# Squares of the rows taken in the expert stage from a second load, no longer tile by tile in attention

## The chip, the core and the metric

The kernel runs on one core of one Trainium2 chip. The time is device microseconds of one execution of the whole program. TensorE (PE) multiplies matrices, VectorE (DVE), ScalarE (ACT) and GpSimd (POOL) work elementwise, SyncE (SP) issues most DMAs. Each engine takes its instructions in the order in which the program lists them.

## What is computed

Sliding-window attention (batch 8, 8 heads, 576 positions, head size 64, window 64), and over its rows a mixture of eight experts that sends each row to one of them:

```python
x = attn_out.transpose(0, 2, 1, 3).reshape(4608, 512)
xn = x / (np.linalg.norm(x, axis=-1, keepdims=True) + 1e-06)
en = expert_emb / (np.linalg.norm(expert_emb, axis=-1, keepdims=True) + 1e-06)
logits = xn @ en.T / tau
expert_idx = np.argmax(logits, axis=1)
gate_w = softmax(logits)[np.arange(N), expert_idx]
h = np.maximum(x[mask] @ w1[e], 0.0)               # 512 -> 1024
out[mask] = gate_w[mask, None] * (h @ w2[e])       # 1024 -> 512
```

The expert is chosen from logits that are not yet divided by the row's norm, since the norm does not move the maximum. The norm, the root of the row's sum of squares, is needed only for the gate.

## The kernel before

Every engine's order is written out by hand. There are two parts that overlap for some 30 us.

**Attention**, 36 tiles of 128 rows, one stage per tile (`stages(s)`), software pipelined: stage s makes the scores of tile s, turns the probabilities of tile s-1, multiplies them with the values for tile s-2, and turns the finished rows of tile s-3. On ScalarE a stage runs, in this order: `own_scores(s)` (L262, a copy from PSUM), the copy of the turned probabilities (`attn_copy`, L295), the copy of the turned rows (`xT_evac`, L384), `squares(s-3)` (L371), at the end of a group of four tiles a small copy of the logits in PSUM (`four_beside`, L416), the issue of a load of keys, and `exponentials(s)` (L276). VectorE merges the scores (L265), takes the maximum (L269), masks probabilities (L298), and divides the rows of tile s-2 (`x_out`, L359 to L363). POOL subtracts the maximum (`less_max`, L273), masks (L301) and scatters finished rows with `place` (L522). In some stages ScalarE and VectorE also split a piece of the first weights (L676, L677).

A finished row is 528 numbers: 512 features, 8 logits (from column `C_LOG`), the sum of squares (`C_SS`) and the token's number (`C_TOK`). `squares(T)` is an activation that writes 512 throw-away values `sq` and leaves their sum in column `C_SS` of the row. `place` writes the rows to DRAM (`xs`), sorted by expert.

**Expert stage**: groups of slots of 128 sorted rows, 39 slots in 13 groups here (kinds E, D, C, F, H with 2, 4, 3, 2 and 1 slots; groups 0 and 1 are E, 2 to 7 are D). Matrices are split into a high and a low half for three passes. For each slot SP loads the 512 features in four DMAs in an order that VectorE can transpose (`load_x`, L890) and the last 16 columns with logits, sum of squares and token into `rest` (`load_rest`, L896). For each group it loads w1 and w2 (`load1` L992, `load2` L1001). In `group(g)` layer 1 runs in parts (8 for a D group); each part's result, in one of four PSUM buffers `ph`, goes through ScalarE's relu to `hh` (L1040) and VectorE's low half `hl` (L1044). Behind the first four parts stands the split of w2 (`renew`, L198 and L201), behind a later part the issue of the next w2 and the gates (`gates`). Layer 2 runs slot by slot (L1084) with the work for the next group between the slots (`ahead`: transposes, split of w1, high and low half of x). `finish` scales a slot's result by its gate on ScalarE (L1109) and scatters it from POOL (L1112); `loads(g + 2)` ends the group.

Gates are made for a batch of slots at once, the first batch being the four slots of groups 0 and 1: `gate_root` (L941) takes the power 0.5 on POOL, `gate_logits` (L947 to L963) is a chain of nine VectorE instructions, `gate_exp` (L968) is on ScalarE, `gate_out` (L978 to L982) again on VectorE. At the seam between attention and experts the order is written line by line (L1284 to L1427): there `gate_root(0)` stands ahead of layer 1 of group 1, and behind the work for group 2 come `gate_logits(0)`, `gate_exp(0)`, `gate_out(0)`, `finish` of group 0's slots, and layer 2 of group 1.

## Time and profile before

| | |
|---|---|
| three runs | 605.72, 606.02, 606.87 us (median 606.02) |
| profiled execution | 605.96 us, span from first to last instruction 604.2 us |
| busy share of the span | TensorE 96%, weight loads 83%, VectorE 60%, ScalarE 48%, POOL 41% |
| mean granted TensorE clock | 0.996 of full speed |
| chain that ended last | TensorE 74%, issue 7%, POOL 6%, VectorE 5%, DMA 4%, ScalarE 3% |

Times in rows are microseconds from the first instruction unless ns stands beside them. `out<-in` are the program's names for tiles, with buffer numbers left out. In a timeline a bracket `[0.52 <-ACT odd L416]` says that the engine was idle for 0.52 us before this instruction and which instruction ended the wait. PEld is TensorE's loading of weights, SPq the sequencer of SP. L with a number is a line of the kernel.

### The profile page before, as it was taken

The numbers are of one execution on the slowest core, as the hardware profiler recorded it, in microseconds if no ns is written. First come the engines' busy times: TensorE is split into PE (matmuls) and PEld (weight loads), VectorE is DVE, ScalarE is ACT, GpSimd is POOL, SyncE is SP. The second block draws the span as 40 slices with busy tenths as digits, with TensorE's granted clock in tenths as the row PEclk, the third lists the DMA queues.
The fourth block names the chain that finished last, engine by engine and source line by source line (L and its number), as shares of the span: only waits on it lengthen the run. The fifth ranks groups of instructions, "written<-read, shape, count | busy, mean of one in ns | idle before, by whom it ended". The sixth has DMA issues, their size and how long they took to land.

```text
span 604.2 us, 16147 instructions
## 1 busy us (share of the span) xinstructions
PE 582.1 (96%) x6198; PEld 500.6 (83%) x6198; DVE 364.1 (60%) x880; ACT 292.5 (48%) x519; POOL 245.0 (41%) x230
## 2 busy tenths in 40 slices
PE   8999998899899999999999999999999999999995
PEld 7888787778889888888888888888888999989984
DVE  5777887888679766166076066166255373728583
ACT  3677776677441464145155145235244363436362
POOL 3558888787822432313214115105204233113221
PEclk9999999999999999999999999999999999999998
DMA  8988988786333796734644554445346455565730
GB/s 281 291 252 269 296 265 290 244 275 190 148 113 135 209 313 199 215 121 123 175 133 136 143 151 141 123 157 173 89 132 204 109 161 145 174 186 178 233 95 23
DMA packets 72471, 110.11 MB, mean 182 GB/s; under 512 B 14773, under 2 KB 34997, under 8 KB 72384
## 3 DMA queue, kind: packets, MB, share of 16 engines
q1 hardware_dynamic: 62080, 80.88, 45.9%
q0 software_dynamic: 6000, 19.18, 8.2%
q10 hardware_dynamic: 4304, 8.93, 4.8%
q8 instruction: 50, 0.82, 0.6%
q14 instruction: 37, 0.30, 0.2%
HBM read 89.69 MB, written 20.05 MB: 182 GB/s over the span
## 4 chain that ended last, share of the span: by engine, by line
PE 74%; issue 7%; POOL 6%; DVE 5%; DMA 4%; ACT 3%; SPq 0%; POOLq 0%; ACTq 0%; DVEq 0%
PE ph L1023 35%; PE po L1084 33%; POOL aM L301 2%; POOL xs L522 2%; DMA out<-o,rest 2%; POOL sm L273 1%; PE back L285 1%; DVE aM L298 1%; DVE xr L363 1%; DVE sm L265 1%; PE odd L321 1%; PE even L335 1%; PE xback L403 1%; PE odd L335 1%; PE score L255 1%
## 5 line engine op out<-in xcount | busy, mean ns | idle before, releaser
L1044 DVE SCALAR_TENSOR_TENSOR hl<-ph,hh 128x512 fp32r<-128x512 f32 (+2 forms) x84 | 54.1, 647 | 154.2 <-ACT hh L1040 154.2
L1023 PE MATMUL ph<-xh,w1h 128*128 128x512 f32 (+2 forms) x384 | 132.5, 345 | 1.3 <-DVE rk L503 1.3
L1023 PE MATMUL ph<-xl,w1h 128*128 128x512 f32 (+2 forms) x384 | 131.9, 344 | 0.0
L1023 PE MATMUL ph<-xh,w1l 128*128 128x512 f32 (+2 forms) x384 | 131.9, 344 | 0.0
L921 POOL TENSOR_TENSOR xl<-xt,xh 128x512 fp32r<-128x512 f32 x37 | 61.8, 1669 | 166.2 <-ACT xh L917 165.8
L1084 PE MATMUL po<-w2l,hh 128*128 128x512 f32 x312 | 121.7, 390 | 0.3 <-DVE w2l L201 0.3
L1084 PE MATMUL po<-w2h,hh 128*128 128x512 f32 x312 | 121.9, 391 | 0.0
L1084 PE MATMUL po<-w2h,hl 128*128 128x512 f32 x312 | 121.6, 390 | 0.0
L1040 ACT ACTIVATE hh<-ph 128x512 fp32r<-128x512 f32 (+2 forms) x84 | 47.5, 566 | 132.9 <-PE ph L1023 121.3
L1112 POOL DMA_INDIRECT out<-o,rest x39 | 43.4, 1112 | 131.4 <-ACT o L1109 106.9
L1023 PEld LDWEIGHTS ph<-xh,w1h 128*128 128x128 f32 x384 | 72.0, 188 | 9.2 <-issue 1.4
L1023 PEld LDWEIGHTS ph<-xl,w1h 128*128 128x128 f32 x384 | 72.1, 188 | 7.9 <-POOL xl L921 0.2
L1023 PEld LDWEIGHTS ph<-xh,w1l 128*128 128x128 f32 x384 | 72.1, 188 | 7.5
L1084 PEld LDWEIGHTS po<-w2l,hh 128*128 128x128 f32 x312 | 58.6, 188 | 13.1 <-DVE w2l L201 1.2
L1084 PEld LDWEIGHTS po<-w2h,hl 128*128 128x128 f32 x312 | 58.6, 188 | 12.3
L1084 PEld LDWEIGHTS po<-w2h,hh 128*128 128x128 f32 x312 | 58.6, 188 | 11.9
L201 DVE TENSOR_TENSOR w1l<-w1raw,w1h 128x1024 fp32r<-128x1024 f32 x44 | 60.4, 1379 | 9.9 <-ACT w1h L198 9.9
L201 DVE TENSOR_TENSOR w2l<-w2raw,w2h 128x1024 fp32r<-128x1024 f32 x48 | 58.8, 1224 | 11.9 <-ACT w2h L198 11.9
L1109 ACT ACTIVATE o<-po,gate 128x512 f32<-128x512 f32 (+1 forms) x39 | 26.5, 684 | 52.4 <-PE po L1084 46.9
L198 ACT CAST w2h<-w2raw 128x1024 fp32r<-128x1024 f32 x48 | 50.1, 1043 | 0.0
L273 POOL TENSOR_TENSOR sm<-sm,st 128x512 f32<-128x512 f32 x36 | 37.4, 1038 | 28.3 <-DVE st L269 26.7
L198 ACT CAST w1h<-w1raw 128x1024 fp32r<-128x1024 f32 x44 | 45.7, 1045 | 3.7 <-DMA w1raw<-in_w 3.7
(225 smaller groups left out, 820.4 us busy)
## 6 DMA issues: line engine op xcount, KB each, us to landing
w2raw<-in_w SPq DMA_DIRECT2D x44, 512.0 KB, 3.8
w1raw<-in_w SPq DMA_DIRECT2D x40, 512.0 KB, 4.4
xb<-xs SPq DMA_DIRECT2D x156, 64.0 KB, 2.2
v<-in_v SPq DMA_DIRECT2D x36, 260.0 KB, 4.1
qT<-in_q SPq DMA_DIRECT2D x36, 256.0 KB, 3.8
kT<-in_k ACTq DMA_DIRECT2D x26, 256.0 KB, 4.2
kT<-in_k SPq DMA_DIRECT2D x10, 256.0 KB, 6.4
w1raw<-in_w SPq DMA_DIRECT2D x8, 256.0 KB, 4.7
```

The costliest lines, as they stand in the source:

```text
L198: nc.scalar.copy(hi[c], raw[c])
L201: eng.tensor_tensor(out=lo[c], in0=raw[c], in1=hi[c].bitcast(F32), op=ALU.subtract)
L273: nc.gpsimd.tensor_tensor(out=t, in0=t, in1=st.pop(T).unsqueeze(2).to_broadcast([P, 8, WIN]), op=ALU.subtract)
L301: nc.gpsimd.tensor_tensor(out=aM[T][:, 0], in0=aM[T][:, 0], in1=halves[:, 0].unsqueeze(1).to_broadcast([P, 4, P]), op=ALU.mult)
L335: nc.tensor.matmul(px[T][hp][pz, u * (D + 1):(u + 1) * (D + 1)], lhsT=mine[pr, u, pz], rhs=vblock(g)[pr, u], start=u == 0 and first[0] and ...
L921: eng.tensor_tensor(out=xl, in0=t, in1=xh.bitcast(F32), op=ALU.subtract)
L1023: nc.tensor.matmul(o, lhsT=ww[c][:, f * P:(f + 1) * P], rhs=xx[:, c, :n], start=(c == 0 and i == 0), stop=(c == 3 and i == 2))
L1040: nc.scalar.activation(hh, ph[g, part][:, :parts(g) * rows_of(g)], AF.Relu)
L1044: nc.vector.scalar_tensor_tensor(out=hl, in0=ph.pop((g, part))[:, :parts(g) * rows_of(g)], scalar=0.0, in1=hh.bitcast(F32), op0=ALU.max, o ...
L1084: nc.tensor.matmul(o, lhsT=xx, rhs=ww[f // 2][:, f % 2], start=(f == 0 and k == 0), stop=(f == 7 and k == 2))
L1109: nc.scalar.activation(o[:, :w], y[:, :w], AF.Copy, scale=gate[:, at:at + 1])
L1112: d = nc.gpsimd.indirect_dma_start(out=out, out_offset=bass.IndirectOffsetOnAxis(ap=tok, axis=0), in_=o, in_offset=None, bounds_check=N - ...
```

## The change

The 36 squares leave the attention stages, and column `C_SS` of the rows is zeroed. In the expert stage each slot's rows are loaded a second time, whole and in plain order, into one of four buffers `xw` (`load_whole`, one DMA of 128 x 512 numbers behind the slot's `load_rest`), and ScalarE squares them from there, with the sum in a small tile `norm` from which the gates read. For group g+1 the squares stand in the second half of group g's layer 1, one behind each part. For the first four slots and the four of group 2 loads and squares stand at the seam, and `gate_root(0)` moves behind them.

```diff
--- before.py
+++ after.py
@@ -365,10 +365,6 @@
     def tokens(G):
         a, b = GROUPS[G]
         nc.gpsimd.tensor_copy(x_rows(a, b)[:, :, C_TOK].bitcast(I32), ct[:, a:b])
-
-    def squares(T):
-        sq = ap.tile([P, DM], BF16, name="sq", bufs=1)
-        nc.scalar.activation(sq, xr[T][:, :DM], AF.Square, accum_out=xr[T][:, C_SS:C_SS + 1])
 
     xT, pxT = {}, {}
 
@@ -633,8 +629,6 @@
         if s - 4 in (28, 29):
             nc.scalar.copy(x_rows(s - 4, s - 3)[:, 0, C_LOG:C_LOG + E], side[(s + 1) % 2][:, :E])
         less_max(s)
-        if there(3):
-            squares(s - 3)
         for G in four:
             four_beside(G)
         load_k(s + RK - 1, nc.sync if s < 6 else nc.scalar)
@@ -895,6 +889,19 @@
         for a in slots:
             note(a, nc.sync.dma_start(rest[:, column(a)], rows(a)[:, DM:ROW]))
 
+    def load_whole(*slots):
+
+        for a in slots:
+            whole[a] = take("xw")
+            note(a, nc.sync.dma_start(whole[a], rows(a)[:, :DM]))
+
+    def squares(*slots):
+
+        for a in slots:
+            nc.scalar.activation(junk, whole.pop(a), AF.Square, accum_out=norm[:, column(a):column(a) + 1])
+
+    whole = {}
+
     def x_turned(a):
 
         b = xb.pop(a)
@@ -937,7 +944,7 @@
         a0, a1 = BATCH[k]
         t, m, t0, t1 = gk[k] = [take("gin")[:, :a1 - a0]] + [take("gsm")[:, :a1 - a0] for _ in range(3)]
         at = slice(column(a0), column(a0) + a1 - a0)
-        gk[k] += [rest[:, at, :E], rest[:, at, C_SS - DM]]
+        gk[k] += [rest[:, at, :E], norm[:, at]]
         nc.gpsimd.tensor_tensor(out=t1, in0=gk[k][5], in1=half.to_broadcast([P, a1 - a0]), op=ALU.pow)
 
     def gate_logits(k):
@@ -1152,6 +1159,7 @@
             for a in SLOT[g]:
                 load_x(a)
             load_rest(*SLOT[g])
+            load_whole(*SLOT[g])
 
     def group(g):
 
@@ -1171,6 +1179,8 @@
                 settle()
             if part == min(4, n - 1) and g + 1 < GS:
                 load2(g + 1)
+            if g + 1 < GS:
+                squares(*SLOT[g + 1][max(0, part - n // 2):][:part >= n // 2])
             if part == min(4, n // 4) and KIND[g] != "H":
                 gates(FIRST[g])
         jobs = ahead(g + 1)
@@ -1194,8 +1204,10 @@
         load1(g)
         load2(g)
         load_rest(*SLOT[g])
+        load_whole(*SLOT[g])
         for a in SLOT[g]:
             x_parts(a)
+        squares(*SLOT[g])
         for c in range(4):
             renew(c, w1raw, w1h, w1l)
         for c in range(4):
@@ -1234,8 +1246,8 @@
     nc.vector.memset(half, 0.5)
     nc.scalar.copy(shift[0], half)
     nc.vector.memset(embT, 0.0)
-    nc.gpsimd.memset(xall[:, :, C_SS + 1:], 0.0)
-    nc.gpsimd.memset(xmore[:, :, C_SS + 1:], 0.0)
+    nc.gpsimd.memset(xall[:, :, C_SS:], 0.0)
+    nc.gpsimd.memset(xmore[:, :, C_SS:], 0.0)
     warm(36)
     expert_norms()
     expert_emb()
@@ -1275,7 +1287,7 @@
     for name, n, shape, dtype in (("gsm", 3, [P, WB], F32), ("gin", 1, [P, WB, E], F32)):
         buffers(name, n, shape, dtype, io)
     rest = io.tile([P, SURE + SIZE["T"], ROW - DM], F32, name="rest")
-    gate = io.tile([P, SURE + SIZE["T"]], F32, name="gate")
+    gate, norm = (io.tile([P, SURE + SIZE["T"]], F32, name=nm) for nm in ("gate", "norm"))
     ring([io.tile([P, DM + i % 2 * SHIFT], F32, name=f"xb{i}")[:, :DM] for i in (2, 3)] + rings["xb"][1], "xb")
     w2h += [io.tile([P, 2, DM], F32R, name=f"w2h{c}") for c in range(4)]
     w2l += [io.tile([P, 2, DM], F32R, name=f"w2l{c}") for c in range(4)]
@@ -1297,7 +1309,6 @@
     maxima(T)
     xT_evac(T - 3)
     less_max(T)
-    squares(T - 3)
     choose(G - 2)
     tokens(G - 2)
     tokens(G - 1)
@@ -1326,7 +1337,6 @@
     x_transposes(T - 2, back)
     values(T - 1)
     xT_evac(T - 2)
-    squares(T - 2)
     tokens(G)
     split_lo(0, w2raw, w2h, w2l, nc.vector)
     x_out(T - 1)
@@ -1349,7 +1359,6 @@
     for x, name in zip(both_hidden, ("hh", "hl")):
         x.append(iob.tile([P, 16 * P], F32R, name=f"{name}1"))
     xT_evac(T - 1)
-    squares(T - 1)
     hidden_hi(0, 2)
     ranks(G - 1)
     split_hi(2, w2raw, w2h)
@@ -1366,7 +1375,6 @@
     x_transposes(T, back)
     logits(T - 1)
     xT_evac(T)
-    squares(T)
     logits(T)
     layer1(0, 7)
     layer2(0, fs=range(1))
@@ -1392,7 +1400,6 @@
     load_x(5)
     load_x(6)
     load_x(7)
-    gate_root(0)
     layer1_part(1, 0)
     split_lo(2, w2raw, w2h, w2l, nc.vector)
     layer1_part(1, 1)
@@ -1411,15 +1418,22 @@
     io2 = ctx.enter_context(tc.tile_pool(name="io2", bufs=1, side="right", reuse_waits="tile"))
     whole_x = [io2.tile([P, 4, 4 * P], F32R, name=f"x{i}") for i in "hl"]
     buffers("o", 4, [P, DM], F32, io2)
+    buffers("xw", 4, [P, DM], F32, io2)
+    junk = io2.tile([P, DM], BF16, name="junk")
     buffers("hr", 2, [P, 2 * P], F32, io2)
     pad(io2, 192)
+    load_whole(*range(EARLY))
     for job in ahead(2):
         job()
+    squares(*range(EARLY))
+    load_whole(*SLOT[2])
+    gate_root(0)
     weave(gate_logits(0))
     gate_exp(0)
     weave(gate_out(0))
     for a in SLOT[0]:
         finish(a)
+    squares(*SLOT[2])
     layer2(1)
     loads(3)
     pending += SLOT[1]
```

## Rows read from the trace of the kernel before

**Rows 1.** Windows of the whole core: busy time of each engine, granted clock, DMA.

```profile
10.00:155.00 145.00, 132.40 (x3614) 114.50 (x3612) 117.33 (x278) 100.98 (x231) 111.36 (x114) 1.00 0.84 266
...
212.00:572.00 360.00, 360.00 (x1722) 307.33 (x1722) 180.40 (x392) 151.25 (x220) 102.15 (x76) 1.00 0.54 162
```

**Rows 2.** Waits of all engines, 10 to 155 us: total us, times, longest.

```profile
ACT sm L276 <- POOL sm L273: 21.3, 25, 1.4
...
DVE sums L359 <- ACT odd L416: 2.1, 4, 0.5
```

**Rows 3.** Line 371, whole span: ns min/median/max, first and last start.

```profile
L371 ACT ACTIVATE sq<-xr x28: 630/644/654, 20.1 to 175.9; 128x512 bf16<-128x512 f32 x28
```

**Rows 4.** Timeline of all engines in a plain stage, 57 to 63 us.

```profile
58.28 0.63 ACT L276 ACTIVATE sm<-sm 128x512 f32<-128x512 f32 x1 [0.59 <-POOL sm L273]
...
62.11 0.63 ACT L276 ACTIVATE sm<-sm 128x512 f32<-128x512 f32 x1 [0.75 <-POOL sm L273]
```

**Rows 5.** Timeline of all engines at the end of a group of four.

```profile
104.11 0.65 ACT L371 ACTIVATE sq<-xmore 128x512 bf16<-128x512 f32 x1
...
104.73 0.21 ACT L416 COPY odd<-even 128x32 f32<-128x32 f32 x1
104.97 0.17 DVE L359 TENSOR_SCALAR sums<-odd 128x8 f32<-128x8 f32 x1 [0.52 <-ACT odd L416]
```

**Rows 6.** Timeline of ScalarE, 205 to 230 us.

```profile
212.71 0.23 ACT L968 ACTIVATE gin<-gin 128x32 f32<-128x32 f32 x1 [3.27 <-DVE gin L963]
213.67 1.27 ACT L1109 ACTIVATE o<-po,gate 128x512 f32<-128x512 f32 x2 [0.73 <-DVE gate L982]
214.83 0.60 ACT L1040 ACTIVATE hh<-ph 128x512 fp32r<-128x512 f32 x1
...
224.47 0.23 ACT L968 ACTIVATE gin<-gin 128x32 f32<-128x32 f32 x1 [2.73 <-DVE gin L963]
```

**Rows 7.** Timeline of SP's DMA issues, 160 to 232 us.

```profile
208.44 2.88 SPq L896 DMA_DIRECT2D rest<-xs  x4
211.89 2.78 SPq L992 DMA_DIRECT2D w1raw<-in_w  x4
215.20 11.86 SPq L890 DMA_DIRECT2D xb<-xs  x16
```

**Rows 8.** Issues of line 896, 207 to 213 us: time from issue to landing.

```profile
DMA to landing us min/median/max: 4.0/4.0/4.0
```

**Rows 9.** Issues of line 890, 240 to 600 us: time from issue to landing.

```profile
DMA to landing us min/median/max: 1.8/2.2/5.1
```

**Rows 10.** Groups by line, whole span: busy us, mean ns, idle before.

```profile
L1044 DVE SCALAR_TENSOR_TENSOR hl<-ph,hh 128x512 fp32r<-128x512 f32 (+2 forms) x84 | 54.1, 647 | 154.2 <-ACT hh L1040 154.2
...
L941 POOL TENSOR_TENSOR gsm<-rest,half 128x4 f32<-128x4 f32 (+3 forms) x12 | 13.9, 1156 | 0.2
```

**Rows 11.** Timeline of VectorE, 160 to 232 us.

```profile
211.35 0.18 DVE L951 TENSOR_TENSOR gin<-rest,gsm 128x32 f32<-128x32 f32 x1
```

**Rows 12.** Chain that ended last: start us, us, what.

```profile
211.99 21.77 PE ph L1023 x96
```

**Rows 13.** Timeline of all engines but weight loads, 572 to 579 us.

```profile
574.71 0.60 ACT L1040 ACTIVATE hh<-ph 128x512 fp32r<-128x512 f32 x1
...
576.13 0.50 PE L1084 MATMUL po<-w2l,hh 128*128 128x512 f32 x1 [0.27 <-DVE w2l L201]
```

**Rows 14.** Windows of one microsecond at the end.

```profile
596.00:597.00 1.00, 0.82 (x4) 0.36 (x2) 0.00 (x0) 0.09 (x1) 0.00 (x0) 1.00 0.00 0
...
598.00:599.00 1.00, 0.00 (x0) 0.00 (x0) 0.00 (x0) 0.00 (x0) 0.82 (x1) 1.00 0.00 0
599.00:600.00 1.00, 0.00 (x0) 0.00 (x0) 0.00 (x0) 0.00 (x0) 0.15 (x1) 0.69 0.38 131
```

**Rows 15.** Line 1040, 255 to 300 us: what ended idle time before it.

```profile
  PE ph L1023: 15.3, 6
```

**Rows 16.** Timeline of SP's DMA issues, 228 to 350 us.

```profile
256.17 3.27 SPq L896 DMA_DIRECT2D rest<-xs  x4
```

## Prediction

> **What bounds the kernel now.** I read the windows first, then the waits of the attention stage, then the timelines of single engines. From 212 to 572 us TensorE is busy 360.00 of 360 us at full clock [rows 1]: the expert stage runs at TensorE's pace, and there ScalarE is busy 151 us of 360. From 10 to 155 us, attention, no engine is full: TensorE 132.4 of 145, VectorE 117.3, POOL 111.4, ScalarE 101.0 [rows 1]. So 12.6 us of TensorE's idle time is all that attention can give back, and ScalarE's share alone says nothing of whether its squares set the pace.
>
> The waits say more. The exponentials of a stage waited for POOL's subtraction in 25 stages, 21.3 us in all [rows 2]: there ScalarE had finished its squares and stood still. In a plain stage one exponential follows the last after 3.83 us, with 0.75 us of waiting for POOL at its end [rows 4]. That loop is exponential, copy of the next scores, VectorE's merge and maximum, POOL's subtraction, exponential again; the square lies in its slack. A few stages differ. Where a group of four tiles ends, ScalarE copies the logits into PSUM behind the square (L416), and VectorE's next instruction waits for that copy: 104.11 the square, 104.73 the copy, 104.97 VectorE, which had been idle 0.52 us [rows 5]. This wait stands 4 times in attention, 2.1 us in all [rows 2].
>
> The change also reaches the seam near 212 us. There ScalarE is an in-order queue of the gates of the first four slots, their output copies and then the first hidden layer of group 2: the exponential at 212.71, two outputs at 213.67, hh of group 2 at 214.83 [rows 6]. TensorE has four hidden buffers. Group 2's layer 1 starts at 211.99 with 21.77 us for 8 parts [rows 12], 2.72 each, so part 4 needs the first buffer back at 222.9. The relu has slack until then.
>
> **The change, part by part.**
>
> *Taken out of attention.* 36 squares of about 644 ns [rows 3]. The next ScalarE instruction starts 0.62 us after a square does (104.11 to 104.73) [rows 5], so 22 us of ScalarE time go. On the path is only the wait of [rows 5] and its like. Of the four waits I take three at 0.5 us; at the fourth I expect the copy of the scores to come next and take the gain. Where VectorE was not idle before it I allow nothing. The last of the three lies close to the first load of sorted rows, which has its own chain through DMA, so I count it as mostly lost and end at **-1.4 us** with a little for the other group ends. Bounds: 0 if the scores' copy always comes next, and 7 group ends by 0.62, -4.3 us. The price is nearest to the measured waits, so 1.4.
>
> *Added loads.* 39 loads of 128 rows of 2 KB, on SP's queue, each after the slots' small loads. In the steady groups SP's small loads end at 259.4 (256.17 + 3.27) [rows 16], four more at 0.72 each (2.88 / 4) [rows 7] end near 262.3 and land near 264.5 by the median landing of 2.2 us [rows 9]. The first square of that group is asked for behind part 4 of group 3. That group starts two layers of 21.8 after 211.99 [rows 12], at 255.6, and part 4 ends 13.6 later, at 269.2. They hold up the next weights' load on SP by less than 3 us, one whole group before these weights are used. Nothing.
>
> *Squares in the expert stage.* 0.62 us each, one behind each of parts 4 to 7. In group 3's two layers ScalarE was idle 15.3 us before its relus, 6 times [rows 15]; 2.5 us a group fit. If that cover were gone, 31 of the 39 would cost some 19 us. They are hidden from group 3 on, but for the last one.
>
> *The seam.* This is where I find the price. The loads of the four early slots stand on SP behind the small loads that end at 211.3 (208.44 + 2.88) [rows 7]. Four issues take them to about 213.2. The small loads just ahead took 4.0 us to land, behind the 2 MB of w2 [rows 8], so the last lands near 217.2 and its square is done near 217.9. Then, in series: POOL's power, which used to run far ahead, 1.16 [rows 10] + 0.1; VectorE's chain, 211.35 to 212.71 in the trace [rows 11, 6] and one instruction more ahead of it, 1.5 + 0.1; then from exponential to hh 2.12 us with the two outputs (212.71 to 214.83) [rows 6]; and four squares of group 2's slots put between, 2.5. hh comes at 217.9 + 1.25 + 1.6 + 2.1 + 2.5 = 225.4, 10.6 us later than before. With its own 0.6 and VectorE's 0.65 [rows 6, 10] the buffer is free at 226.7, and TensorE stands from 222.9: **+3.8 us**. Behind the waiting squares on ScalarE stand all relus of group 2 and its w2 casts; nothing else feeds TensorE. Bounds by the landing: 1.8 and 5.1 [rows 9] give 1.6 and 4.9.
>
> *The backlog behind it.* hh of part 3 stands behind the exponential of the next gates. In the trace that came 9.64 us after hh of part 0 (214.83 to 224.47), 2.73 of it waiting for VectorE [rows 6]. With three casts, two outputs and the gates' chain packed I reckon 8.8, so part 7 can start near 235.7, and TensorE, from 226.7, asks at 234.9: **+0.8 us** (0 to 0.8).
>
> *The clock.* After TensorE's last matmul at 596.8 the granted clock is 1.00 until 599 and 0.69 in the next microsecond [rows 14]: idle for over 2 us, it fell towards the lower level, 1.2 GHz. An idle stretch of 3.8 us in mid-kernel may do so too, and no row shows how soon the clock comes back after one. I bound it by none, and by the whole of part 4 at half speed, 2.7 us, of which the 0.8 above hides as much: 0 to +1.9. Between them, **+0.6**. The Trainium skill, "TensorE: Matmul & The Clock Gate", section "Why this matters for your kernels", warns against idle gaps between bursts of matmuls, since the clock must be earned again by activity; the fall at the end of the trace agrees, the return is shown by no run here. By that rule the sum would be at its far end, 1.3 us above mine.
>
> *The last square.* In group 11 ScalarE is late: hh of the last part at 574.71, and TensorE waits 0.27 us for VectorE's w2 half at 576.13 [rows 13]. The single slot of group 12 has its square put ahead of that hh, 0.62 us: **+0.5** (0 to 0.6).
>
> *SP behind the seam.* The second four loads wait for the first four squares, so SP's load of w1 for group 3 starts near 218.7 and not at 211.89, its 16 row loads end near 234 (11.86 us long), the small ones near 237.4, and the loads for group 3's squares are issued from 237.6 to 240 [rows 7], landing from 239.8 to 242. ScalarE reaches the first of these squares near 236 and stands there, with relus 5 to 7 behind it. Layer 2 wants relu 5 at 234.9 + 0.8 + 2.7 + 3.4 = 241.8, which is about when VectorE's half of it is done. I count 0, with no margin. The two zeroings that are one column wider and the new small tiles cost nothing: they lie before the first tile's wait.
>
> **Sum.** -1.4 + 3.8 + 0.8 + 0.6 + 0.5 = +4.3 us on the profiled execution's 605.96 us: **610.3**. That execution stands 0.06 below the median of 606.02, so the same number holds for the median. What a measurement of this kernel can tell from no change is about 0.2%, 1.2 us.
>
> **The rivals.**
>
> *A. ScalarE was the bound of attention after all: faster.* All four engines there are at 70 to 91%, so any of them freed may shorten the loop more than one execution's waits show. The price: TensorE's idle 12.6 us [rows 1] is the most. It decides once attention gives more than the 5.7 us of the other terms and the 1.2 of the measurement, 6.9 us. With 9 us it ends at 602.7. Against it: the 25 waits for POOL, and no wait for a square [rows 2].
>
> *B. Gain and stall cancel: no change.* The early loads land after 1.8 us, and all seven group ends give something: -3 + 1.6 + 0.8 + 0.5, 605.9.
>
> *C. A second stall.* The loads for group 3's squares land after 5.1 us instead of 2.2 and layer 2 of group 2 waits 2.9 us more: 613.2. For it: nothing is left over in the reckoning above. Against: 2.2 is the median of 108 such landings, 5.1 the worst.
>
> *D. The clock stays low through part 4.* The rule cited above, as a mechanism of this kernel: part 4 at half speed, 2.7 us, 0.8 hidden: 611.6.
>
> **How the numbers follow.** My forecast (seam 3 to 5 us, attention 1 to 2) 0.50; D 0.14; C 0.16; A 0.13; B 0.07. Slower by over 0.2% is the forecast with C and D and a little of B: 0.81. Within: 0.06. Faster: 0.13. The likeliest time is 610.3, its own range 608.3 to 612.3. For 8 in 10, A and the lower half of B are left out, about 0.16, and above the far ends of C and D together, so 606.3 to 614.3.
>
> **What would show it.** In the changed profile: no square in attention, and L416's waits gone or halved; the four plain waits for POOL as before, with the 3.83 us loop. TensorE idle for the first time in the expert stage, some 4 us near 221 (1.4 earlier than here), released by VectorE's hl behind ScalarE's hh; ScalarE waiting for the early rows' DMA and then for the gates; hh of group 2 some 10 us after layer 1 began where it was 3. The granted clock below 1.00 there or not decides D. ScalarE waiting for DMA before squares in parts 4 to 7 of group 2 decides C; layer 1 and 2 of group 3 back at 21.8 us each says that the steady groups hide their squares. Wrong would be: no idle TensorE at the seam (the loads earlier than I place them), or attention shorter by over 3 us.

## The result, and the profile after

The changed kernel takes 613.60 us (median of 4 runs, 612.50 to 617.05) against 605.87 us (median of 4 runs, 605.31 to 606.87) of the kernel before: a ratio of 1.0135, 95% interval 1.0092 to 1.0179. It is slower by 7.7 us. The profiled execution took 612.93 us with a span of 611.1, 6.9 more than the span before. Lines have moved by up to 7: L1023 is now L1030, L1040 L1047, L1044 L1051, L1084 L1091, L1109 L1116, L416 L412; the new square is L901 and the new load L896.

The windows of the whole core (columns as in [rows 1]) say where not to look:

```profile
10.00:155.00 145.00, 132.90 (x3607) 114.71 (x3605) 117.36 (x278) 81.54 (x167) 111.09 (x115) 1.00 0.84 265
...
212.00:245.00 33.00, 28.72 (x116) 22.22 (x114) 13.02 (x35) 17.89 (x40) 6.65 (x6) 0.95 0.76 231
...
263.00:580.00 317.00, 317.00 (x1537) 271.98 (x1536) 159.92 (x344) 147.68 (x243) 86.57 (x64) 1.00 0.57 175
```

In attention ScalarE is busy 81.5 us where it was 101.0 [rows 1], and TensorE is as busy as before. From 263 us on TensorE has no gap, with 27 of the 39 squares added there. The missing time lies from 212 to 263 us. The first matmul of each layer, in TensorE's timelines of both kernels, gives the whole account:

| stretch | before, us | after, us | difference |
|---|---|---|---|
| start to layer 1 of group 2 | 211.83 | 211.65 | -0.18 |
| layer 1 of group 2, parts 0 to 3 and the wait | 10.88 | 14.98 | +4.10 |
| its parts 4 to 7 | 10.88 | 12.58 | +1.70 |
| layer 2 of group 2 | 21.80 | 23.63 | +1.83 |
| group 3 through layer 1 of group 11 | 317.34 | 317.19 | -0.15 |
| layer 2 of group 11 to the last output copy | 24.17 | 24.34 | +0.17 |
| from there to the end | 7.27 | 6.72 | -0.55 |
| sum | 604.2 | 611.1 | +6.9 |

(10.88 is half of layer 1's 21.77.) ScalarE's timeline of the changed kernel shows the seam, to be read against [rows 6]:

```profile
214.59 0.63 ACT L901 ACTIVATE junk<-xw 128x512 bf16<-128x512 f32 x1 [6.64 <-DMA xw<-xs]
...
216.86 0.63 ACT L901 ACTIVATE junk<-xw 128x512 bf16<-128x512 f32 x1
...
220.27 0.23 ACT L975 ACTIVATE gin<-gin 128x32 f32<-128x32 f32 x1 [2.69 <-DVE gin L970]
221.23 1.27 ACT L1116 ACTIVATE o<-po,gate 128x512 f32<-128x512 f32 x2 [0.73 <-DVE gate L989]
222.39 0.63 ACT L901 ACTIVATE junk<-xw 128x512 bf16<-128x512 f32 x1
...
225.27 0.58 ACT L1047 ACTIVATE hh<-ph 128x512 fp32r<-128x512 f32 x1
...
241.80 0.63 ACT L901 ACTIVATE junk<-xw 128x512 bf16<-128x512 f32 x1 [5.81 <-DMA xw<-xs]
242.43 0.57 ACT L1047 ACTIVATE hh<-ph 128x512 fp32r<-128x512 f32 x1
243.07 0.63 ACT L901 ACTIVATE junk<-xw 128x512 bf16<-128x512 f32 x1
243.71 0.58 ACT L1047 ACTIVATE hh<-ph 128x512 fp32r<-128x512 f32 x1
```

ScalarE stands 6.6 us for the early rows, then for VectorE's gates; the relu of group 2 starts at 225.27, 10.4 us later than before. Far below, the squares of group 3 stand between the last relus of group 2. TensorE's timeline answers to both places:

```profile
222.31 0.39 PE L1030 MATMUL ph<-xh,w1l 128*128 128x512 f32 x1
...
226.63 0.80 PE L1030 MATMUL ph<-xh,w1h 128*128 128x512 f32 x1 [3.94 <-DVE hl L1051]
...
242.38 0.39 PE L1091 MATMUL po<-w2h,hl 128*128 128x512 f32 x1
243.06 0.50 PE L1091 MATMUL po<-w2h,hh 128*128 128x512 f32 x1 [0.29 <-ACT hh L1047]
...
244.33 0.50 PE L1091 MATMUL po<-w2h,hh 128*128 128x512 f32 x1
...
245.43 0.50 PE L1091 MATMUL po<-w2h,hh 128*128 128x512 f32 x1
```

The 3.94 us is the stall that the prediction looked for. At 243 us layer 2 takes 1.1 to 1.3 us for the three matmuls of one hidden block, which otherwise take 0.68 (three at 0.227). One row names 0.29 us of waiting there, yet the layer is 1.83 us longer: the record of a matmul, 0.39 to 0.50 us, is longer than the 0.227 us between two starts at full pace, so starts that come 0.33 to 0.55 us apart list hardly any idle time. Only starts set against starts show it. Windows of one microsecond show what the idle stretch did to the clock (the third number from the right):

```profile
225.00:226.00 1.00, 0.00 (x0) 0.00 (x0) 0.12 (x1) 1.00 (x4) 0.00 (x0) 1.00 1.00 307
226.00:227.00 1.00, 0.37 (x1) 0.37 (x2) 0.76 (x2) 1.00 (x2) 0.00 (x0) 0.81 0.97 303
227.00:228.00 1.00, 1.00 (x3) 0.79 (x3) 1.00 (x1) 1.00 (x3) 0.35 (x1) 0.50 1.01 369
...
229.00:230.00 1.00, 1.00 (x4) 0.81 (x3) 0.75 (x2) 1.00 (x3) 0.81 (x1) 0.50 1.07 352
230.00:231.00 1.00, 1.00 (x5) 0.83 (x5) 1.00 (x2) 0.81 (x1) 1.00 (x2) 0.99 0.74 228
```

It was still granted whole in 225 to 226, when TensorE had stood for three microseconds, and fell to 0.50, the 1.2 GHz level, about when it started again: one matmul then follows another after 0.43 us and not after 0.23, until 230. SP's queue answers to [rows 7]:

```profile
207.45 2.90 SPq L890 DMA_DIRECT2D rest<-xs  x4
210.47 7.94 SPq L896 DMA_DIRECT2D xw<-xs  x8
218.92 1.92 SPq L999 DMA_DIRECT2D w1raw<-in_w  x4
221.40 13.72 SPq L884 DMA_DIRECT2D xb<-xs  x16
235.64 2.90 SPq L890 DMA_DIRECT2D rest<-xs  x4
239.11 3.03 SPq L896 DMA_DIRECT2D xw<-xs  x4
```

The second four loads stand until the squares free their buffers, and the loads for group 3 leave 6 to 8 us later than before. In attention the waits (columns as in [rows 2]) are not those I expected:

```profile
ACT sm L276 <- POOL sm L273: 33.2, 25, 2.0
...
ACT odd L412 <- PE odd L335: 2.0, 5, 0.4
...
DVE sums L359 <- ACT odd L412: 1.5, 4, 0.4
```

ScalarE's wait for POOL has grown from 21.3 to 33.2 us, as fits squares that lay in slack. But the copy at a group's end, which used to wait for the square, now waits for TensorE's matmuls into its bank, and VectorE waits for the copy 1.5 us in all where it was 2.1 [rows 2].

### The profile page after: what moved, and what is told of

Same layout as the page of the kernel before. It is cut to its first block, busy times and chain, and to the rows that moved or that the text cites. A ratio compares the mean times of both kernels' runs of the same rounds, so it can differ in the third digit from the quotient of the medians.

```text
span 611.1 us, 16194 instructions
## 1 busy us (share of the span) xinstructions
PE 585.7 (96%) x6198; PEld 501.6 (82%) x6198; DVE 366.8 (60%) x880; ACT 295.3 (48%) x525; POOL 245.6 (40%) x230
## 4 chain that ended last, share of the span: by engine, by line
PE 62%; issue 10%; POOL 8%; DVE 7%; DMA 6%; SPq 2%; ACT 2%; POOLq 0%; ACTq 0%; DVEq 0%
PE po L1091 28%; PE ph L1030 28%; POOL xs L518 3%; POOL aM L301 3%; DMA out<-o,rest 2%; SPq L884 2%; POOL sm L273 2%; DMA xb<-xs 2%; DMA w1raw<-in_w 1%; PE back L285 1%; PE score L255 1%; DVE sm L265 1%; DVE aM L298 1%; PE even L335 1%; PE odd L335 1%
## 5 line engine op out<-in xcount | busy, mean ns | idle before, releaser
L1051 DVE SCALAR_TENSOR_TENSOR hl<-ph,hh 128x512 fp32r<-128x512 f32 (+2 forms) x84 | 54.1, 648 | 152.6 <-ACT hh L1047 152.6
L1030 PE MATMUL ph<-xh,w1h 128*128 128x512 f32 (+2 forms) x384 | 133.4, 347 | 5.2 <-DVE hl L1051 3.9
L1030 PE MATMUL ph<-xl,w1h 128*128 128x512 f32 (+2 forms) x384 | 132.5, 345 | 0.0
L1030 PE MATMUL ph<-xh,w1l 128*128 128x512 f32 (+2 forms) x384 | 132.3, 345 | 0.0
L1091 PE MATMUL po<-w2h,hh 128*128 128x512 f32 x312 | 122.2, 392 | 0.3 <-ACT hh L1047 0.3
L1091 PE MATMUL po<-w2l,hh 128*128 128x512 f32 x312 | 121.7, 390 | 0.6 <-DVE w2l L201 0.6
L1091 PE MATMUL po<-w2h,hl 128*128 128x512 f32 x312 | 121.8, 391 | 0.0
L1047 ACT ACTIVATE hh<-ph 128x512 fp32r<-128x512 f32 (+2 forms) x84 | 47.4, 566 | 113.6 <-PE ph L1030 102.6
L1119 POOL DMA_INDIRECT out<-o,rest x39 | 45.1, 1156 | 130.1 <-ACT o L1116 106.0
L1030 PEld LDWEIGHTS ph<-xh,w1h 128*128 128x128 f32 x384 | 72.5, 189 | 13.5 <-DVE hl L1051 4.4
L1030 PEld LDWEIGHTS ph<-xl,w1h 128*128 128x128 f32 x384 | 72.5, 189 | 8.0 <-POOL xl L928 0.2
L1030 PEld LDWEIGHTS ph<-xh,w1l 128*128 128x128 f32 x384 | 72.5, 189 | 7.7
L1091 PEld LDWEIGHTS po<-w2h,hl 128*128 128x128 f32 x312 | 58.5, 188 | 13.4 <-DVE hl L1051 1.3
L1091 PEld LDWEIGHTS po<-w2l,hh 128*128 128x128 f32 x312 | 58.6, 188 | 13.2 <-DVE w2l L201 1.4
L1091 PEld LDWEIGHTS po<-w2h,hh 128*128 128x128 f32 x312 | 58.6, 188 | 12.9 <-ACT hh L1047 1.3
L201 DVE TENSOR_TENSOR w1l<-w1raw,w1h 128x1024 fp32r<-128x1024 f32 x44 | 63.1, 1441 | 8.6 <-ACT w1h L198 8.3
L1116 ACT ACTIVATE o<-po,gate 128x512 f32<-128x512 f32 (+1 forms) x39 | 26.4, 684 | 47.8 <-PE po L1091 47.1
```

What stands on the lines that cost most here:

```text
L201: eng.tensor_tensor(out=lo[c], in0=raw[c], in1=hi[c].bitcast(F32), op=ALU.subtract)
L1030: nc.tensor.matmul(o, lhsT=ww[c][:, f * P:(f + 1) * P], rhs=xx[:, c, :n], start=(c == 0 and i == 0), stop=(c == 3 and i == 2))
L1047: nc.scalar.activation(hh, ph[g, part][:, :parts(g) * rows_of(g)], AF.Relu)
L1051: nc.vector.scalar_tensor_tensor(out=hl, in0=ph.pop((g, part))[:, :parts(g) * rows_of(g)], scalar=0.0, in1=hh.bitcast(F32), op0=ALU.max, o ...
L1091: nc.tensor.matmul(o, lhsT=xx, rhs=ww[f // 2][:, f % 2], start=(f == 0 and k == 0), stop=(f == 7 and k == 2))
L1116: nc.scalar.activation(o[:, :w], y[:, :w], AF.Copy, scale=gate[:, at:at + 1])
```

## The experiments

The theory: the loss is made in one place, 212 to 247 us, as an in-order chain (early rows, squares, gates, outputs, more squares, relu), the clock's fall behind the stall, and a second wait in layer 2; attention gives little. The rivals: the 39 loads and squares cost time wherever they stand; or attention gives much and the expert stage costs still more. Times stand beside runs of the kernel before on the same chip, with medians of 606.01 us (first eight kernels) and 606.91 us (last four).

**The gain alone.** The kernel before without its squares in attention:

```
-        if there(3):
-            squares(s - 3)
```

> The kernel before with the 36 squares of attention left out and nothing put in their place (the norms read zeros, so the gates' values are not the reference's; that part of the computation is left out). It times the gain alone. Seam theory (the loss is made at one place, 212 to 246 us, and attention gives little): 605.2 to 605.9, that is 0.0 to 0.7 us below the kernel before, since where a group of four tiles ends L416 then waits for TensorE's matmuls into the same bank instead of for the square. My prediction's term of 1.4 us: 604.5. Rival (attention gives several us and the expert stage costs over 10): 603 or less.

605.33 us, ratio 0.9985, interval 0.9956 to 1.0015: by this -2.7 to +0.9 us. Nothing large is to be had. Why one trace can't say more is seen in the subtraction's line, from the third tile to the 34th (first and last start are the last numbers), in the changed kernel:

```profile
L273 POOL TENSOR_TENSOR sm<-sm,st x32: 1032/1036/1044, 14.8 to 146.7; 128x512 f32<-128x512 f32 x32
```

and in the second kernel with extra matmuls below, which has none there either:

```profile
L273 POOL TENSOR_TENSOR sm<-sm,st x32: 1032/1035/1045, 14.7 to 144.7; 128x512 f32<-128x512 f32 x32
```

131.9 and 130.0 us with the same attention code; the 11 profiles with attention as in the changed kernel or in this one lie between 130.0 and 133.5, median 131.2, and the one trace of before has 131.7. The plain stages are 3.82 us in all of them; the scatter lies in the stages where a group of four ends.

**The seam, first try.** Three kernels moved group 3's squares, the third the whole seam. All three had a fault of mine: the squares of group 3 stood in the program behind the loads that reuse their four buffers. They read group 4's rows (group 3's gates come out of those) and waited for them.

```
-            if g + 1 < GS:
+            if g > 2 and g + 1 < GS:
                 squares(*SLOT[g + 1][max(0, part - n // 2):][:part >= n // 2])
+            if g == 3 and part == 0:
+                squares(*SLOT[3])
```

(The second adds the matmuls shown further below; the third has nearly the order of the late seam, below.)

> The changed kernel, but the four squares of group 3's slots stand behind the first relu of group 3 and no longer between the relus of group 2. Only the second wait is undone, the one in layer 2 of group 2. Seam theory with three separate terms (stall 3.9, clock 1.6, second wait 1.7): 1.7 us less than the changed kernel, some 611.2 to 611.9, TensorE without idle time from 239 to 247 us, group 3 starting 5.7 us later than in the kernel before instead of 7.4. Rival (what is taken away there is waited for elsewhere, since ScalarE's backlog of relus and casts is the cause and not the squares' rows): same as the changed kernel, 612.9 to 613.6.

> The kernel of the run before in this list, with 16 extra matmuls into the buffer of part 3 of group 2 ahead of its own twelve, 3.6 us of work that fills the stretch in which TensorE stands idle for group 2's relu (their sums are overwritten). Seam theory: the granted clock stays at 1.00, part 4 takes 2.72 us instead of 4.4, and the time falls by 1.6 us below the run before, to 609.6 to 610.3. Rival (the matmuls of part 4 are slow because their operands come late or the profile shows the clock only in the records, or the slow part is hidden behind the next relus): no change against the run before, 611.2 to 611.9.

> The changed kernel with the seam put in another order and nothing left out: the early slots' squares stand behind the relu of part 1 of group 2, their gates behind part 2, the outputs of groups 0 and 1 behind part 3; the loads of group 2's whole rows stand on SP behind all loads of group 3, their squares and gates behind part 7; group 3's loads behind those and its squares behind part 0 of group 3. Seam theory: the stall, the slow clock and the second wait all go, and the time is that of the kernel before less what attention gives, 605.2 to 606.2. Rival (39 loads and squares cost something wherever they stand, by traffic or by ScalarE's time in the steady groups): 608 or more, with the groups from 4 on longer than 21.8 us a layer.

612.57 us (ratio 1.0108, interval 1.0074 to 1.0142), 616.54 (1.0158, 1.0112 to 1.0205) and 617.30 (1.0176, 1.0140 to 1.0213). By time a rival would have won with the third. Its trace says otherwise: layers 1 and 2 of group 2 take 21.76 us each, without a gap; the loss is in group 3, where ScalarE's queue shows my fault,

```profile
275.38 0.63 ACT L901 ACTIVATE junk<-xw 128x512 bf16<-128x512 f32 x1 [13.54 <-DMA xw<-xs]
```

and TensorE's waits from 212 to 575 us what it costs:

```profile
PE ph L1030 <- DVE hl L1051: 9.6, 1, 9.6
PE ph L1030 <- POOL xl L928: 1.5, 1, 1.5
```

The four were done again in the right order (the fourth is group 2's squares, below).

**The second wait, and the clock.**

```
-            if g + 1 < GS:
+            if g > 2 and g + 1 < GS:
                 squares(*SLOT[g + 1][max(0, part - n // 2):][:part >= n // 2])
...
+        if g == 2:
+            squares(*SLOT[3])
         if g + 1 < GS and KIND[g + 1] == "H":
             gates(FIRST[g + 1])
         loads(g + 2)
```

> The changed kernel, but the four squares of group 3's slots stand at the end of group 2, behind its output copies and ahead of the loads that reuse their buffers, and no longer between group 2's relus. Only the second wait is undone. Seam theory with separate terms: layer 2 of group 2 takes 21.8 us again, group 3 starts 1.7 us earlier against the end of the seam's stall than in the changed kernel, the time is 611.2 to 611.9 if the early rows land as in the changed kernel's profile. Rival (the backlog of relus and casts is the cause): layer 2 of group 2 still waits 1 us or more, 612.9 to 613.6.

```
         o = ph[g, f // per][:, f % per * n:(f % per + 1) * n]
+        if (g, f) == (2, 3):
+            for i in range(16):
+                nc.tensor.matmul(o, lhsT=w1h[0][:, f * P:(f + 1) * P], rhs=xh[:, 0, :n], start=i == 0, stop=i == 15)
```

> The kernel ahead of it in this list with 16 extra matmuls into the buffer of part 3 of group 2 ahead of its own twelve (3.6 us, their sums are overwritten), in the stretch where TensorE waits for the relu. Seam theory: the clock stays at 1.00 and nothing else moves, 1.6 us below the kernel ahead of it: 609.6 to 610.3, and from the end of the wait to layer 2 of group 2 about 10.9 us (four parts at 2.72) where it is 12.5. Rival (the clock costs nothing): the same as the kernel ahead of it.

613.57 us (1.0111, 1.0066 to 1.0156) and 611.26 (1.0083, 1.0057 to 1.0108). Both lie above what was expected. The medians differ by 2.3 us, in the way expected of the clock, but the intervals overlap, and the first is no faster than the changed kernel. The traces tell more, by starts of ScalarE's squares and relu and of TensorE's parts and layers, in us from the start of group 2's layer 1:

| kernel | first early square | first relu | part 4 starts | part 4 to layer 2 | layer 2 |
|---|---|---|---|---|---|
| changed kernel | 2.94 | 13.62 | 14.98 | 12.58 | 23.63 |
| group 3's squares later (first try) | 4.01 | 14.70 | 16.06 | 12.46 | 21.76 |
| group 3's squares later | 3.92 | 14.60 | 15.95 | 13.66 | 21.76 |
| the same with matmuls (first try) | 3.25 | 13.94 | 15.30 | 11.57 | 21.75 |
| the same with matmuls | 4.13 | 14.82 | 16.18 | 11.56 | 21.76 |
| group 2's squares spread | 1.67 | 9.49 | 10.88 | 11.49 | 21.76 |
| late seam | none ahead | 2.91 | 10.88 | 10.88 | 21.76 |

Three things are shown. Layer 2 takes 21.76 us as soon as the squares leave the relus: the second wait is real, 1.87 us. The relu starts 10.68 to 10.69 us after the first early square wherever that falls, and part 4 another 1.36 behind it: when the rows land moves the whole seam one for one. And they land differently from run to run, 2.9 to 4.1 us into the layer in the first five traces; why is not shown. That scatter can hide much of the 1.8 us in the timed runs, and a larger one lies ahead of the seam. At the end of attention TensorE waits 1.27 us for VectorE in all 14 profiled executions. In nine the clock stays whole, as in the changed kernel,

```profile
153.00:154.00 1.00, 0.35 (x1) 0.19 (x1) 0.75 (x3) 0.00 (x0) 1.00 (x2) 1.00 0.08 29
154.00:155.00 1.00, 0.97 (x8) 0.97 (x9) 0.00 (x0) 0.00 (x0) 1.00 (x2) 1.00 0.00 0
```

and layer 1 of group 2 starts 64.8 to 65.0 us after POOL's 34th subtraction. In five, both kernels of this pair among them, it falls; in the one with the extra matmuls:

```profile
151.00:152.00 1.00, 0.35 (x1) 0.19 (x1) 0.76 (x3) 0.00 (x0) 1.00 (x2) 0.93 0.23 88
152.00:153.00 1.00, 0.98 (x5) 0.97 (x5) 0.00 (x0) 0.00 (x0) 1.00 (x2) 0.50 0.02 8
...
161.00:162.00 1.00, 1.00 (x24) 0.88 (x16) 0.00 (x0) 1.00 (x3) 0.98 (x1) 0.50 0.00 0
```

There layer 1 starts 66.2 to 69.4 us after it. Up to there the two programs are the same, so this fall comes and goes from execution to execution. The timed runs of the kernel with the matmuls part by their mean granted clock: seven at 0.995 or more took 609.66 to 611.72 us, four at 0.991 or less 612.55 to 615.55.

Ahead of part 4, the clock in the kernel without the extra matmuls,

```profile
232.00:233.00 1.00, 0.29 (x1) 0.29 (x2) 0.76 (x2) 1.00 (x2) 0.00 (x0) 0.50 0.96 314
...
237.00:238.00 1.00, 1.00 (x3) 0.71 (x3) 1.00 (x2) 0.00 (x0) 0.62 (x1) 0.50 0.93 337
238.00:239.00 1.00, 1.00 (x5) 0.82 (x4) 0.97 (x6) 0.00 (x0) 0.00 (x0) 0.80 0.62 156
```

and in the one with them:

```profile
229.00:230.00 1.00, 0.00 (x0) 0.00 (x0) 0.46 (x1) 1.00 (x3) 0.00 (x0) 1.00 1.07 328
230.00:231.00 1.00, 0.71 (x3) 0.63 (x4) 0.76 (x2) 1.00 (x3) 0.00 (x0) 1.00 0.90 333
```

In the first TensorE stood 4.9 us and the clock is at 0.50 from 232 to 238; in the second it stands 1.5 us and the clock stays at 1.00. Parts 4 to 7 then take 11.56 us, 0.7 more than without a stall: the backlog, most of it at part 6 (3.14 us and not 2.72). In the changed kernel part 4 takes 4.42 us and parts 5 to 7 take 2.72 each, so all of its 1.70 us are the slow clock, which hid the backlog; to hold the clock would give back 1.0. In the kernel without the extra matmuls it would give back 2.1, yet on the first try, after a wait of 5.0 us, only 0.9: there the clock was at 0.50 for three microseconds. The length of the wait alone does not set how long the clock stays down.

**Group 2's squares out of the chain.** On the first try group 3's rows were loaded into the buffers ahead of these squares (group 2's gates came out of group 3's rows): 626.39 us, ratio 1.0317, interval 1.0282 to 1.0352, TensorE idle 16.4 us.

> The kernel at the head of this list, with the four squares of group 2's slots moved from ahead of group 2's first relu to behind its first four relus, one each, and group 2's gates from part 2 to part 4. Seam theory (everything on ScalarE ahead of that relu counts one for one): the stall falls by 3.0 us (four squares at a pitch of 0.75), from 3.9 to about 0.9 if the early rows land as in the changed kernel's profile, the clock stays at 1.00, and the time is some 4.6 us below the head of the list: 606.6 to 607.5. Rival (the relu waits for the rows and the gates alone): stall and time as at the head of the list.

Again, with group 3's loads behind:

```
-            load_whole(*SLOT[g])
+            if g > 3:
+                load_whole(*SLOT[g])
...
+            if g == 2 and part < 4:
+                squares(SLOT[2][part])
+            if part == (4 if g == 2 else min(4, n // 4)) and KIND[g] != "H":
                 gates(FIRST[g])
...
+        if g == 2:
+            load_whole(*SLOT[3])
+            squares(*SLOT[3])
...
-    squares(*SLOT[2])
     layer2(1)
```

> The changed kernel with group 3's whole rows and squares at the end of group 2 (no second wait), and the four squares of group 2's slots moved from ahead of group 2's first relu to behind its first four relus, one each, group 2's gates from part 2 to part 4. The early slots' squares, gates and outputs stay ahead of the relu. Seam theory (all that stands on ScalarE ahead of that relu counts one for one): from the first early square to the first relu 7.7 us instead of 10.7, idle TensorE ahead of part 4 some 1 to 2 us instead of 3.9 to 5, the clock at 1.00 throughout, 607.0 to 609.0 us. Rival (the relu waits for the rows and the gates alone, the squares fit beside): wait as in the changed kernel, 611.5 to 613.5.

608.17 us, ratio 1.0025, interval 0.9998 to 1.0051. ScalarE's timeline:

```profile
213.44 0.63 ACT L901 ACTIVATE junk<-xw 128x512 bf16<-128x512 f32 x1 [6.23 <-DMA xw<-xs]
...
221.26 0.60 ACT L1047 ACTIVATE hh<-ph 128x512 fp32r<-128x512 f32 x1
```

7.8 us from the first square to the relu, where it was 10.7: 2.9 us less, which is what the four squares took in the changed kernel (222.39 to 225.27), one for one. The rows landed early in this execution (1.67 us into the layer), so there is no gap at all ahead of part 4; the timed runs reach from 605.84 to 612.63 us.

**The late seam.** Nothing is left out; the chain stands behind the relus.

```
+            if g == 3:
+                load_whole(*SLOT[2])
             for a in SLOT[g]:
                 load_x(a)
             load_rest(*SLOT[g])
-            load_whole(*SLOT[g])
+            if g > 3:
+                load_whole(*SLOT[g])
...
-            if part == 0:
+            if part == (3 if g == 2 else 0):
                 settle()
...
-            if g + 1 < GS:
+            if g > 2 and g + 1 < GS:
                 squares(*SLOT[g + 1][max(0, part - n // 2):][:part >= n // 2])
...
+            if g == 2 and part == 1:
+                squares(*range(EARLY))
+                loads(3)
+            if g == 2 and part == 2:
+                gates(0)
+            if g == 2 and part >= 4:
+                squares(SLOT[2][part - 4])
+            if part == (7 if g == 2 else min(4, n // 4)) and KIND[g] != "H":
                 gates(FIRST[g])
...
+        if g == 2:
+            load_whole(*SLOT[3])
+            squares(*SLOT[3])
...
-    squares(*range(EARLY))
-    load_whole(*SLOT[2])
-    gate_root(0)
...
-        finish(a)
-    squares(*SLOT[2])
     layer2(1)
-    loads(3)
-    pending += SLOT[1]
+    pending += SLOT[0] + SLOT[1]
```

> The changed kernel with the seam in another order and nothing left out: the early slots' squares stand behind the relu of part 1 of group 2, their gates behind part 2, the outputs of groups 0 and 1 behind part 3; group 2's whole rows are loaded behind group 3's first weights, their squares stand behind parts 4 to 7 and the gates behind part 7; group 3's whole rows and squares at the end of group 2. Seam theory: no idle TensorE in groups 2 and 3, all steady groups at 21.8 us a layer, 605.0 to 606.2, the time of the kernel before less what attention gives. Rival (39 loads and squares cost something wherever they stand): 608 or more.

605.41 us, ratio 0.9985, interval 0.9961 to 1.0008, and the same 39 loads and squares. Its window to [rows 1]:

```profile
212.00:572.00 360.00, 360.00 (x1727) 307.58 (x1726) 185.85 (x405) 175.17 (x298) 102.93 (x77) 1.00 0.61 190
```

No gap, no slow clock, ScalarE busy 24 us more. The time is that of the kernel with no squares at all (605.33). The loss was the order of the seam; the rival that puts it on the work falls.

**Twice the work in the steady groups.** On the late seam, each load and square from group 4 on stands twice.

> The kernel with the late seam (605.4 us), but from group 4 on each slot's whole rows are loaded twice and squared twice: 27 loads of 256 KB and 27 squares more, some 20 us of ScalarE time. If the steady groups hide this work with room to spare: 605.0 to 606.5, all their layers at 21.8 us. Rival (traffic or ScalarE's time there costs something already): 607 or more, a loss that shows as layers longer than 21.8 us.

609.49 us, ratio 1.0058, interval 1.0027 to 1.0089: a miss. From group 3's start to layer 1 of group 11 it is 2.95 us longer than the late seam's trace. Layer 2 of group 3 takes 23.1 us. ScalarE and TensorE there:

```profile
279.63 0.63 ACT L904 ACTIVATE junk<-xw 128x512 bf16<-128x512 f32 x1 [1.60 <-DMA xw<-xs]
...
281.02 0.58 ACT L1050 ACTIVATE hh<-ph 128x512 fp32r<-128x512 f32 x1
```

```profile
281.65 0.50 PE L1094 MATMUL po<-w2h,hh 128*128 128x512 f32 x1 [0.79 <-ACT hh L1050]
```

It is the second wait again: a square that stands for its rows, a relu behind it, layer 2 behind the relu. Another 2.2 us lie in layer 2 of group 11 (14.4 us where the late seam's trace has 12.2), where TensorE waits for the halves of w2 from ScalarE and VectorE, with a second square of the last slot in ScalarE's queue ahead of a cast. One set is hidden; a second one is not.

**Is the freed time of use?** In eight stages of attention a cast of w1 stands on ScalarE between the exponential and the next copy. Moved ahead of the exponential, in the kernel before and in the late seam:

```
+        if s in wsplit:
+            c, at = wsplit[s]
+            nc.scalar.copy(w1h[c][:, at], w1raw[c][:, at])
         if s > 2:
             exponentials(s)
```

> The kernel before with one line moved in attention: in the 8 stages that split a piece of the first w1, ScalarE's cast stands ahead of the exponential and not behind it. ScalarE waits there for POOL with nothing to do, while VectorE's subtraction and the copy of the next scores wait for the cast. If attention's pace is the loop exponential, copy, merge, maximum, subtraction, each of these stages falls from 4.46 to some 3.85 to 4.0 us, in all 3 to 5 us: 601.0 to 603.0. If ScalarE's own time is the bound as long as its squares stand there, or TensorE is: 605 to 606.

> The kernel with the late seam (605.4 us) with the same move of the cast as in the kernel ahead of it in this list. Here ScalarE waits 1.4 to 2.0 us for POOL in such a stage, so the cast fits whole: 3 to 5 us less, 600.4 to 602.4. If squares in attention and the cast's place are worth the same slack, the two kernels come out alike within 1 us; if the squares stood in the cast's way, this one is faster by over 1 us.

605.97 us (0.9986, 0.9962 to 1.0010) and 604.20 (0.9962, 0.9924 to 1.0000). Neither gave the 3 to 5 us. The second is the best median of all, 2.7 us under the kernel before, and its interval just reaches no change; the two kernels' intervals overlap. Such a stage fell from 4.46 to 4.36 us only, in both. VectorE and POOL in the first of the two kernels:

```profile
99.31 1.27 POOL L301 TENSOR_TENSOR aM<-aM,cs 128x512 f32<-128x512 f32 x1
...
99.77 1.37 DVE L678 TENSOR_TENSOR w1l<-w1raw,w1h 128x512 fp32r<-128x512 f32 x1
```

VectorE's subtraction, now earlier, stands beside a POOL instruction and takes 1.37 us where it took 0.69 (1.18 to 1.37 in the eight stages of this kernel); the merge behind it comes hardly sooner. In these stages what the move won in waiting it lost there. Whether the freed time is of use without that is not shown.

## Why the prediction was right or wrong

Slower was right, and the range of 606.3 to 614.3 held the 613.6; the likeliest time of 610.3 was 2.6 us under the profiled 612.93, and its own range ended at 612.3. The two large misses are the second wait (0 forecast, +1.83) and the gain in attention (1.2 us too much). By its steps:

- *Taken out of attention, -1.4.* -0.18 in the profiled execution, where a lead of 0.98 us at the fourth tile, half of it from the first, was down to 0.11 at 90 us; the first square of before starts only at 20.1 us [rows 3], about when the fourth tile's subtraction does, so this lead is not the squares'. "At three of the four waits 0.5 us" failed in its mechanism: without the square the copy of L412 waits for TensorE (2.0 us, five times), and VectorE's wait for it fell by 0.6 us in all. Timed alone it is -0.7 with an interval that holds -1.4 and 0. The true size stays open: one execution scatters more.
- *The seam, +3.8.* +4.10. Step by step: last early square done 217.9 (217.59), relu 225.4 (225.27), TensorE again 226.7 (226.63). (The relu came 13.62 us after layer 1 began; the "some 10 us" among the signs does not go with the reckoning above it, which has 13.4.) The four squares put between cost 2.88 us and not 2.5 (0.75 each back to back), and the early rows and the gates came 0.5 us sooner than reckoned. The chain is shown by the one-for-one moves of the table and by the kernels without it. That the sum came so close is partly luck: the early rows landed anywhere from 1.7 to 4.1 us into the layer in the seven executions with them in this place.
- *Backlog 0.8 and clock 0.6.* +1.70 for both, all of it in part 4 at the low clock; with the clock held a backlog of 0.7 is left. Rival D had the mechanism, a slow part 4 that hides the backlog, and the size too high: eight of the part's twelve matmuls were slow, 1.70 us and not 2.7. The Trainium skill, "TensorE: Matmul & The Clock Gate", section "Why this matters for your kernels", which warned of idle gaps between bursts: the trace agrees, with 0.50 for three microseconds after 3.94 us of waiting.
- *SP behind the seam, 0 "with no margin".* This is the step that failed: +1.83. The loads were issued from 239.1 to 242.1 and not from 237.6 to 240, the first square started at 241.80, and the relu of part 5 stood behind it, a second stall as in rival C. Its 613.2 is close by luck: it took the stall from a landing of 5.1 us, and here the loads left 1.5 us late. What I had not reckoned is that the wait goes on: with a square behind each relu ScalarE gives one hidden block in 1.1 to 1.3 us, and layer 2 asks for one in 0.68. I compared a single relu's time with its due time, and not the two rates.
- *The last square, +0.5.* +0.17 for its layer and the outputs; TensorE waits 0.57 us for w2 in two places where it waited 0.27 in one [rows 13].
- *Steady groups, nothing.* -0.15. Right, but twice the work costs 3 us there in the trace, so the cover is not the idle time of ScalarE alone: when the rows land counts.

The end after the last output was 0.55 us shorter in the execution after; nothing in the change bears on it, and the cause is open. Why the timed difference is 7.7 us and the profiled 6.9 is not shown: landings scatter by over two microseconds and count one for one, and the fall of the clock at the end of attention, which the profiled execution escaped, cost 1.3 to 4.5 us where it came.

## What to carry to other kernels

Work moved off a busy-looking engine is not free where it goes: before asking whether the engine has time, ask what stands behind the new instruction in its queue, and from where its data comes. A chain that hangs on data just written and loaded again belongs behind the instructions that feed the bottleneck, not ahead of them; that order was worth the whole loss here. Where two streams share an in-order engine, compare the rate at which it delivers with the rate asked for, not the due time of the first piece.

## What the runs showed of the hardware

- An idle stretch of TensorE can cost twice. In the waits ahead of part 4 the granted clock fell to 0.50 about a microsecond or less before their end, and stayed down when TensorE worked again: matmuls of 128x512 follow each other in 0.427 us and not in 0.227, for 3 to 4 us after 3.94 and after 5.01 us of waiting, and 5.5 after 4.91.
- A short wait can cost the clock too, and not in every execution. Behind the same wait of 1.27 us at the end of attention the clock fell to 0.50 for some 3 to 10 us in five of 14 profiled executions, which cost 1.3 to 4.5 us, and stayed at 1.00 in nine. What decides is not shown.
- A ScalarE square with an accumulated sum is two instructions, 0.63 and 0.19 us; back to back a pair takes 0.75, with a relu or a copy behind it 0.61 to 0.63.
- VectorE's 128x512 subtraction of two tiles in SBUF took 1.37 us beside a POOL multiplication of 1.27 us, and 0.69 where it ran behind it. The Trainium skill, "SBUF — State Buffer", section "Who interferes with whom", says that a VectorE instruction with two SBUF inputs and a GpSimd instruction that reads SBUF contend; this row agrees.
